# A recurrent attention and feed-forward kernel: a fifth slice of d_ff in plain float32, and a new order for the first 42 tasks

## The chip, the cores and the metric

The kernel runs on one core of a Trainium2 chip. The metric is the device time of one execution in microseconds (us). TensorE (PE) multiplies matrices into PSUM, VectorE (DVE) and ScalarE (ACT) work elementwise, GpSimd (POOL) does little here, and SyncE (SP) issues most of the DMA transfers.

## The reference

```python
# attention: r, k, v, w are (4, 8, 768, 48), u is (8, 48)
for t in range(S):
    cur = np.einsum('bhd,bhe->bhde', u[None] * kt, vt)
    y[:, :, t] = np.einsum('bhd,bhde->bhe', rt, state + cur)
    state = wt[:, :, :, None] * state + np.einsum('bhd,bhe->bhde', kt, vt)
# feed-forward on x = y as (3072 tokens, 384), d_ff = 2048
h = x @ w_in
g = h * (1.0 / (1.0 + np.exp(-1.702 * h)))
return (g @ w_out).astype(np.float32)
```

## The kernel before, in words

The 3072 tokens are 24 chunks of 128. A chunk `t` goes through 13 stages (`chunk`, written `a<t>` in the order below; each mention of the token runs one more stage):

1. DVE: a scan (L330) and a reciprocal; 2. DVE: a second scan (L335); 3. DVE: one multiplication that makes `kq` (L341); 4. PE: transposes of `k` (L348), ACT copies them out (`kt`, L350); 5. DVE: `rku` (L356, chunks 0 to 7) or three operations on `rk_t` (L359 to L361, later chunks); 6. PE: `ps_d` (L368, chunks 0 to 7); 7. ACT (chunks 0 to 7) or DVE makes `am`; 8. PE: `ps_u` (L398, L402); 9. the state: DVE, in a sequence's first chunk ACT copies `mid` first (L406); 10. DVE: two predicated copies into `am` (L415); 11. and 12. PE: `ps_y` (L425, L438), with a one-element copy between (L448); 13. ACT and DVE write the rows of `x`, as a high and a low half.

The feed-forward part is cut into 106 tasks, each a group of chunks by one slice of 128 columns of d_ff. `g<j>` is the first product of task j (PE, L502 to L504), `h<j>` its gelu (two activations on ACT, L519 and L520, and the subtraction `gl` on DVE, L522), `y<j>` its second product (PE, L540 to L542). Tasks 0 to 4 take slices 0 to 4 for the first pair of chunks (256 tokens), tasks 5 to 9 the same slices for the second pair, tasks 10 to 19 slices 5 to 9 for the two pairs in turn; from task 20 on a task has four chunks (512 tokens).

Ordinarily a number is split into two float32r halves and each product is three matmuls (high by high, low by high, high by low). For the tasks in `PLAIN` the product is one float32 matmul on the unsplit weights and an unsplit copy of `x` (`xw`, L497 and L537), and `h` is one activation on ACT with nothing on DVE.

The weights come in 12 pieces. `f<i>` fetches piece i (SP), and `w<i>` has four stages: 1. ACT: two activations (L253, L254); 2. DVE: two integer operations (L256, L259), after which the piece is a usable float32; 3. ACT: the high half (L263); 4. DVE: the low half (L267). Even pieces belong to the first product, odd ones to the second; pieces 0 to 3 hold slices 0 to 4 and a part of 5. The staging tile `st` has three buffers, so `f<i>` waits for stage 2 of `w<i-3>`.

`l<t>` loads chunk t's inputs on SP (chunk 0's second part on ACT's queue; later chunks also `rk_t`), `M` loads a small mask, `m<t>` is a measurement on ACT (L277), `x1`, `x3`, `x7` rearrange rows of `x` by DMA (L481, SP and POOL), `s0` splits `xw` for the tasks that are not plain, `u` loads one more constant. `d<n>` puts n matmuls on a constant tile (L305, 128x512 bf16) ahead of the next PSUM bank's real work; their results are overwritten.

Every engine runs its instructions in the order in which they were written, and that order is one string by hand, `RAMP`. It holds all work up to the second product of task 39, the gelu of task 41 included. After it `rest` orders what is left by a rule; that part is the same in both kernels, because both strings hold the same tokens (only the `d` differ). The edit is in two constants: `PLAIN`, which `plain` reads (L487), and `RAMP`, which the first of these loops reads.

```python
TASKS = [(0, c, c + 2, f) for c in (0, 2) for f in range(5)]
PLAIN = range(4)
for token in RAMP.split():
    do(token)
for token in rest():
    do(token)
```

Of the kernel before, what the change touches and what calls it, by code (L numbers as in the profile page):

```python
# [71 lines left out]

PLAIN = range(4)
WHOLES = range(2)
PARTS = [("a", -2, 2, 7), ("a", -1, 1, 7), ("a", 0, 1, 6), ("a", 1, 0, 5), ("a", 1, 1, 4),
         ("a", 1, 1, 7), ("a", 1, 2, 0), ("a", 1, 2, 3), ("a", 1, 2, 7), ("m", 1, 2, 7), ("a", 2, 1, 1),
# [1 line left out]
BEFORE = 9  # L80
FIRST = 42
RAMP = """
l0 l1 M l0 a0 a0 a0 f0 m0 d36 a0 a0 a0 a0 a1 a1 a1 m1 l0 d11 a0 a0 a0 w0 l2 a1 a1 d5 a1 a1 a2 f1 w1 w0 l1 d9 a1 a1
a1 a2 a0 l3 f2 a0 a2 a0 l3 a1 m2 d4 a2 a1 a1 a2 w2 a2 a2 a3 a3 l2 d9 a2 a3 x1 a3 a3 w1 m3 f3 a2 a3 g0 g1 h0 a3 w2 a2
y0 h1 a3 l4 a3 w3 f4 a3 a2 w1 f5 w2 a4 g2 a3 h2 a4 a2 w3 a3 w0 a2 a3 g3 s0 h3 a4 y1 y2 y3 w4 a4 a4 s0 a4 w2 w0 w4 a4
l5 l4 a4 g4 x3 h4 w3 w3 g5 w1 g6 g7 h5 g8 a5 w5 h6 w4 y4 y5 f6 f7 w4 g9 h7 w5 g10 w6 y6 a4 h8 y7 y8 w7 w6 h9 g11 w5
g12 y9 w5 h10 a5 f8 f9 g13 w6 h11 y10 y11 m4 a5 h12 w7 g14 l6 w6 l5 w8 f10 h13 a5 a5 y12 g15 g16 m5 h14 a4 h15 y13
a6 a5 w7 y14 y15 h16 g17 g18 w7 w9 y16 g19 w8 f11 h17 y17 w9 w8 h18 a6 w8 a5 h19 a4 l6 a5 w9 a5 a4 a6 a5 g20 w9 w10
h20 a6 y18 w10 w11 a6 w11 g21 h21 g22 l7 m6 y19 w10 w10 y20 w11 w11 a6 l8 a7 h22 a5 a4 l8 a7 a6 y21 a5 a7 a6 u g23
a6 l7 a6 a7 a7 l9 a8 h23 a7 a5 a7 g24 a6 l9 a7 a8 a7 a6 a8 m7 a7 a9 l10 a9 y22 a8 y23 a6 h24 a7 a8 a8 m8 a8 a8 a7 a7  # L90
a9 x7 g25 a8 h25 y24 y25 a9 a9 a10 g26 a8 l11 a10 a9 a9 a8 h26 l10 a9 a8 a10 m10 l12 a8 g27 a10 a9 a10 m9 h27 a11 a9
g28 g29 h28 a10 y26 h29 a9 a10 a11 l11 a10 a10 a9 a11 y27 y28 a10 a11 a11 y29 a11 a11 a9 m11 l13 a11 a11 a11 a10 a11
a10 a12 a11 a10 g30 a11 g31 g32 h30 h31 y30 a12 a12 m12 a13 g33 a12 h32 y31 y32 l14 g34 g35 g36 g37 a13 a13 h33 g38
h34 g39 h35 g40 y33 y34 h36 g41 h37 y35 y36 h38 y37 h39 h40 y38 h41 y39
"""
WIDE = 512
GAP = 64
# [7 lines left out]
def rwkv_ffn_kernel(ctx: ExitStack, tc, wkr, vp, vrk, ub, w_in, w_out, masks, vt, uc, out):  # L105
# [379 lines left out]
    def plain(j):  # L485

        return j in PLAIN  # L487

# [312 lines left out]
```

## Time and profile before

| | us |
|---|---|
| three runs | 510.77, 509.82, 505.54 |
| median | 509.82 |
| the profiled execution | 505.89 |
| its span, first to last instruction | 504.2 |
| outside the span | 1.7 |

The profile is one execution. Rows of a time line give the start, the duration, the engine (a `q` behind it is its sequencer, for instance a DMA issue), the line, the operation and the tiles (out, then in), the count, and in brackets the idle time of that engine just before with what ended it. Neighbouring instructions of one engine overlap a little, so from one start to the next is shorter than the duration.

### The profile page before, as it was taken

To read this page: it belongs to the slowest core of one execution; us is meant where nothing else is said; L and a number is where in the kernel's file an instruction comes from. 1 tells how busy PE (TensorE), PEld (TensorE's weight loads), DVE (VectorE), ACT (ScalarE), POOL (GpSimd) and SP (SyncE) were. 2 spreads that over 40 slices of the span, in tenths; PEclk is the share of its full clock that TensorE was granted. 3 is DMA by queue.
4 is the path that set the end of the run, shared out by engine and by line. 5 is a ranking of instruction groups with operands and counts; after the bars stand their busy time and mean duration, and the time that the engine had idled before them with its cause. 6 is when DMAs were issued, how large, how long until landed. Compare 5 with 4: busy or idle time off the path is not lost.

```text
span 504.2 us, 11925 instructions
## 1 busy us (share of the span) xinstructions
PE 492.4 (98%) x5064; PEld 406.1 (81%) x5064; DVE 294.8 (58%) x503; ACT 227.3 (45%) x527; POOL 15.4 (3%) x48
## 2 busy tenths in 40 slices
PE   9997999999999999999999999999999999999995
PEld 4676999887778888888888888888888878888884
DVE  8798999999896403755655555655555521111211
ACT  2897998865634313542342433342442432322221
POOL 2011000001001000000001000001000001000000
PEclk9999999999999999999999999999999999999999
DMA  8868586443731600171104071204040001100002
GB/s 222 252 185 228 171 211 192 107 128 109 214 105 24 167 0 2 63 219 45 55 1 126 17 213 61 59 1 128 2 156 1 1 1 31 64 0 1 0 0 72
DMA packets 26510, 45.84 MB, mean 91 GB/s; under 512 B 3952, under 2 KB 17712, under 8 KB 26448
## 3 DMA queue, kind: packets, MB, share of 16 engines
q1 hardware_dynamic: 25472, 42.94, 29.5%
q0 software_dynamic: 864, 1.66, 1.4%
q8 instruction: 42, 0.69, 0.6%
q10 hardware_dynamic: 112, 0.39, 0.3%
q14 instruction: 20, 0.16, 0.1%
HBM read 38.00 MB, written 4.72 MB: 85 GB/s over the span
## 4 chain that ended last, share of the span: by engine, by line
PE 89%; DVE 6%; DMA 2%; issue 1%; SPq 0%; ACT 0%; DVEq 0%
PE po L540 12%; PE ph L502 12%; PE ph L504 12%; PE ph L503 12%; PE po L542 12%; PE po L541 12%; PE ps_y L425 2%; PE ps_y L438 2%; PE ps_u L402 2%; PE ps_t L305 2%; PE ps_u L398 2%; PE ps_t L348 1%; PE ps_d L368 1%; DVE am L415 1%; DVE lp L335 1%
## 5 line engine op out<-in xcount | busy, mean ns | idle before, releaser
L522 DVE TENSOR_TENSOR gl<-gf,gh 128x512 fp32r<-128x512 f32 (+1 forms) x102 | 66.1, 648 | 160.4 <-ACT gf L520 159.2
L519 ACT ACTIVATE gh<-ph 128x512 fp32r<-128x512 f32 (+1 forms) x102 | 57.7, 566 | 204.6 <-PE ph L504 185.6
L502 PE MATMUL ph<-x,h 128*128 128x512 f32 (+1 forms) x306 | 116.1, 379 | 0.0
L504 PE MATMUL ph<-x,l 128*128 128x512 f32 (+1 forms) x306 | 114.2, 373 | 0.0
L503 PE MATMUL ph<-x,h 128*128 128x512 f32 (+1 forms) x306 | 114.1, 373 | 0.0
L540 PE MATMUL po<-gh,h 128*128 128x512 f32 (+1 forms) x300 | 114.0, 380 | 0.0
L542 PE MATMUL po<-gl,h 128*128 128x512 f32 (+1 forms) x300 | 112.2, 374 | 0.8 <-DVE gl L522 0.8
L541 PE MATMUL po<-gh,l 128*128 128x512 f32 (+1 forms) x300 | 111.9, 373 | 0.0
L504 PEld LDWEIGHTS ph<-x,l 128*128 128x128 f32 x306 | 57.6, 188 | 10.4
L542 PEld LDWEIGHTS po<-gl,h 128*128 128x128 f32 x300 | 56.5, 188 | 11.6 <-DVE gl L522 1.6
L502 PEld LDWEIGHTS ph<-x,h 128*128 128x128 f32 x306 | 57.7, 188 | 9.9
L503 PEld LDWEIGHTS ph<-x,h 128*128 128x128 f32 x306 | 57.7, 189 | 9.5
L540 PEld LDWEIGHTS po<-gh,h 128*128 128x128 f32 x300 | 56.5, 188 | 10.3
L541 PEld LDWEIGHTS po<-gh,l 128*128 128x128 f32 x300 | 56.6, 189 | 9.3
L520 ACT ACTIVATE gf<-ph 128x512 f32<-128x512 f32 (+1 forms) x102 | 57.3, 562 | 3.0 <-DVE gl L522 2.9
L330 DVE TENSOR_TENSOR_SCAN lp<-wkr_t,d1r 112x516 f32<-112x516 f32 x24 | 29.4, 1227 | 0.9 <-DMA wkr_t<-in_wkr 0.9
L335 DVE TENSOR_TENSOR_SCAN lp<-wkr_t,d1f 112x516 f32<-112x516 f32 x24 | 29.5, 1230 | 0.5
L341 DVE TENSOR_TENSOR kq<-wkr_t,lp 112x1024 f32<-112x1024 f32 x24 | 29.3, 1220 | 0.7 <-PE ps_y L438 0.3
L277 ACT ACTIVATE junk<-lp 112x1032 bf16<-112x1032 f32 x24 | 25.6, 1066 | 7.2 <-DVE lp L335 7.2
L350 ACT COPY kt<-ps_t 128x448 f32<-128x448 f32 (+1 forms) x24 | 12.7, 531 | 32.2 <-PE ps_t L348 32.0
L438 PE MATMUL ps_y<-kq,mid 64*64 64x64 f32 (+3 forms) x384 | 23.0, 218 | 3.4 <-issue 2.4
L438 PEld LDWEIGHTS ps_y<-kq,mid 48*48 48x48 f32 (+3 forms) x384 | 18.5, 127 | 4.6 <-issue 2.9
(102 smaller groups left out, 508.5 us busy)
## 6 DMA issues: line engine op xcount, KB each, us to landing
st<-in_w_out SPq DMA_DIRECT2D x6, 1024.0 KB, 6.3
rk_t<-in_vrk SPq DMA_DIRECT2D x16, 384.0 KB, 3.9
st<-in_w_in SPq DMA_DIRECT2D x6, 896.0 KB, 7.0
v_t<-in_vrk SPq DMA_DIRECT2D x24, 192.0 KB, 3.5
out_t<-ob SPq DMA_DIRECT2D x15, 256.0 KB, 2.2
wkr_t<-in_wkr SPq DMA_DIRECT2D x18, 192.0 KB, 2.9
wkr_t<-in_wkr SPq DMA_DIRECT2D x36, 96.0 KB, 3.5
wkr_t<-in_wkr SPq DMA_DIRECT2D x5, 577.9 KB, 6.4
```

The costliest lines, as they stand in the source:

```text
L330: V.tensor_tensor_scan(li[:, ::-1], w1[:, ::-1], d1r.rearrange("r p c -> r (p c)")[:, ::-1], 0.0, op0=ALU.mult, op1=ALU.add)
L335: V.tensor_tensor_scan(pm, w0, d1f.rearrange("r p c -> r (p c)"), 0.0, op0=ALU.mult, op1=ALU.add)
L438: T.matmul(ps[b][head(h), p], from_[head(half), p * D + OFF * h : p * D + HB], qf[head(half), p, blocks[b]], start=False, stop=p == PAIRS[ ...
L502: T.matmul(ph, h_, xs[i][:, 0, c, cs], start=c == 0, stop=False)
L503: T.matmul(ph, h_, xs[i][:, 1, c, cs], start=False, stop=False)
L504: T.matmul(ph, l_, xs[i][:, 0, c, cs], start=False, stop=c == NM - 1)
L519: A.activation(gh, ph, AF.Gelu_apprx_sigmoid, scale=1.0 / W_SCALE)
L520: A.activation(gf, ph, AF.Gelu_apprx_sigmoid, scale=1.0 / W_SCALE)
L522: V.tensor_tensor(gl, gf, gh.bitcast(F32), op=ALU.subtract)
L540: T.matmul(o, h_, gh, start=first, stop=False, skip_group_check=True)
L541: T.matmul(o, l_, gh, start=False, stop=False, skip_group_check=True)
L542: T.matmul(o, h_, gl, start=False, stop=f == NF - 1, skip_group_check=True)
```

## The change

`PLAIN` goes from four tasks to five, so task 4 (slice 4, first pair of chunks) becomes a plain float32 task. `RAMP` is another sequence of the same 395 working tokens. The constant matmuls go from 36 + 11 + 5 + 9 + 4 + 9 = 74 to 26 + 6 + 6 + 5 + 4 + 5 = 52. In the diff the beginning, a middle part and the end of the two strings:

```diff
-PLAIN = range(4)
+PLAIN = range(5)
 RAMP = """
-l0 l1 M l0 a0 a0 a0 f0 m0 d36 a0 a0 a0 a0 a1 a1 a1 m1 l0 d11 a0 a0 a0 w0 l2 a1 a1 d5 a1 a1 a2 f1 w1 w0 l1 d9 a1 a1
-a1 a2 a0 l3 f2 a0 a2 a0 l3 a1 m2 d4 a2 a1 a1 a2 w2 a2 a2 a3 a3 l2 d9 a2 a3 x1 a3 a3 w1 m3 f3 a2 a3 g0 g1 h0 a3 w2 a2
-y0 h1 a3 l4 a3 w3 f4 a3 a2 w1 f5 w2 a4 g2 a3 h2 a4 a2 w3 a3 w0 a2 a3 g3 s0 h3 a4 y1 y2 y3 w4 a4 a4 s0 a4 w2 w0 w4 a4
...
-g28 g29 h28 a10 y26 h29 a9 a10 a11 l11 a10 a10 a9 a11 y27 y28 a10 a11 a11 y29 a11 a11 a9 m11 l13 a11 a11 a11 a10 a11
-a10 a12 a11 a10 g30 a11 g31 g32 h30 h31 y30 a12 a12 m12 a13 g33 a12 h32 y31 y32 l14 g34 g35 g36 g37 a13 a13 h33 g38
...
+l0 M l1 l0 a0 a0 a0 d26 a0 l0 a1 a0 d6 a0 f0 m0 a0 a0 l2 a1 l1 a1 l2 a0 a1 m1 a1 d6 a1 l3 a1 a0 a2 a1 a0 a1 a0 a1 w0
+l3 a2 a1 a0 a2 a3 d5 a2 a1 a1 f1 w1 f2 x1 a2 a3 d4 a2 a3 a2 a2 l4 a3 a2 a3 d5 a3 w0 f3 a3 a3 a2 a3 m2 a3 g0 h0 g1 w2
+l4 w1 a2 h1 a3 w2 a4 a2 f4 w3 a2 w2 w3 a3 a3 x3 y0 y1 w2 g2 g3 h2 w1 h3 f5 g4 w0 h4 a4 s0 y2 w4 w0 y3 y4 m3 g5 s0 a4
+w4 h5 w3 w1 a4 w3 a4 w5 g6 h6 g7 g8 g9 l5 w5 h7 y5 f6 w4 l6 f7 w4 a4 a4 a4 h8 a5 w5 y6 f8 w5 y7 h9 a5 w6 g10 g11 g12
...
+a7 m7 a6 m6 a8 g24 a7 a7 a5 a8 y22 a7 h24 a6 a7 a7 a6 a7 l8 a8 y23 l9 a7 a6 a8 l9 a8 m8 a8 a7 l10 a9 a8 l10 a8 a7 a7
+a9 x7 a9 g25 y24 h25 y25 a9 a9 a8 a8 a10 a10 g26 g27 h26 y26 a9 a9 l11 h27 a8 a9 a9 m9 a8 a10 g28 a11 y27 a9 a10 a10
+a10 a10 g29 a8 a11 h28 a9 a10 l11 a9 a11 h29 y28 a10 a11 y29 g30 a11 a9 a11 m10 a10 a11 a11 a11 a11 h30 l12 a10 a11
...
```

## Rows read from the trace of the kernel before

**Rows 1.** The page: busy time of each engine over the whole span.

```profile
PE 492.4 (98%) x5064; PEld 406.1 (81%) x5064; DVE 294.8 (58%) x503; ACT 227.3 (45%) x527; POOL 15.4 (3%) x48
```

**Rows 2.** Windows: stretch, length, busy (instructions) by engine, granted clock, DMA share, GB/s.

```profile
0.00:5.00 5.00, 3.86 (x10) 1.38 (x11) 2.97 (x5) 1.49 (x2) 3.13 (x24) 1.00 0.63 168
5.00:10.00 5.00, 5.00 (x23) 2.22 (x22) 4.64 (x6) 1.16 (x2) 0.00 (x0) 1.00 1.02 266
40.00:45.00 5.00, 2.57 (x77) 2.08 (x78) 4.86 (x5) 1.76 (x5) 0.00 (x0) 1.00 1.06 311
60.00:80.00 20.00, 19.70 (x166) 19.50 (x165) 19.80 (x31) 18.57 (x39) 0.00 (x0) 1.00 0.70 182
140.00:155.00 15.00, 14.22 (x343) 11.60 (x342) 12.66 (x30) 4.34 (x12) 0.00 (x0) 1.00 0.23 71
155.00:201.00 46.00, 46.00 (x230) 37.63 (x225) 17.13 (x26) 15.88 (x35) 1.50 (x3) 1.00 0.21 52
180.00:200.00 20.00, 20.00 (x90) 16.56 (x89) 3.77 (x6) 6.52 (x12) 0.00 (x0) 1.00 0.01 1
```

**Rows 3.** Time line of DVE, the end of chunk 11's stage 10.

```profile
152.62 0.76 DVE L415 COPY_PREDICATED am<-after,ps_u 128x256 f32<-128x256 int32 x2
```

**Rows 4.** Time line of DVE, chunks 0 and 1: first scan, `rku`, second `kq`, state.

```profile
5.25 1.23 DVE L330 TENSOR_TENSOR_SCAN lp<-wkr_t,d1r 112x516 f32<-112x516 f32 x1 [0.94 <-DMA wkr_t<-in_wkr]
...
9.14 0.68 DVE L356 TENSOR_TENSOR rku<-wkr_t 112x512 f32<-112x512 f32 x1
12.49 1.23 DVE L341 TENSOR_TENSOR kq<-wkr_t,lp 112x1024 f32<-112x1024 f32 x1
16.33 0.36 DVE L412 TENSOR_TENSOR sf<-ps_u,mid 112x192 f32<-112x192 f32 x1 [2.61 <-ACT mid L406]
```

**Rows 5.** Time line of PE: the first constant matmuls and what follows them.

```profile
1.14 10.11 PE L305 MATMUL ps_t<-warm 128*128 128x512 bf16 x36 [1.14 <-DVE warm L119]
11.09 0.55 PE L348 MATMUL ps_t<-ident,kq 112*128 112x112 f32 x4
```

**Rows 6.** Time line of ACT, 8 to 16 us.

```profile
8.07 1.06 ACT L277 ACTIVATE junk<-lp 112x1032 bf16<-112x1032 f32 x1 [5.29 <-DVE lp L335]
11.68 0.53 ACT L350 COPY kt<-ps_t 128x448 f32<-128x448 f32 x1 [2.45 <-PE ps_t L348]
...
12.73 2.02 ACT L378 ACTIVATE am<-same,s 128x64 f32<-128x64 f32 x8
14.66 1.05 ACT L277 ACTIVATE junk<-lp 112x1032 bf16<-112x1032 f32 x1
15.98 0.32 ACT L406 COPY mid<-ps_u 112x192 f32<-112x192 f32 x1 [0.18 <-PE ps_u L402]
```

**Rows 7.** Time line of SP's queue: chunk 1's load and the mask.

```profile
1.29 0.41 SPq L198 DMA_DIRECT2D wkr_t<-in_wkr  x1
2.80 0.31 SPq L617 DMA_DIRECT2D hm<-in_masks  x1
```

**Rows 8.** The instructions of one line: whole loads of a chunk, from issue to landing.

```profile
DMA to landing us min/median/max: 4.6/6.4/11.0
```

**Rows 9.** Time line of PE and DVE, 43 to 56 us: waits before the split tasks begin.

```profile
43.92 0.25 PE L438 MATMUL ps_y<-kq,mid 48*48 48x64 f32 x1 [2.43 <-issue]
46.25 1.49 DVE L272 TENSOR_TENSOR x<-ps_y,x 112x256 fp32r<-112x256 f32 x4 [1.28 <-ACT x L271]
55.95 2.36 DVE L267 TENSOR_TENSOR l<-h,h 128x1024 fp32r<-128x1024 f32 x2 [0.51 <-ACT h L263]
```

**Rows 10.** Time line of DVE: chunk 10's `rk_t` operations begin.

```profile
137.54 0.56 DVE L359 TENSOR_TENSOR rk_t<-rk_t 128x384 f32<-128x384 f32 x1 [1.56 <-DMA rk_t<-in_vrk]
```

**Rows 11.** The chain that ended last, pieces in time: start, duration, what.

```profile
46.86 3.88 PE po L537 x18
53.57 0.12 PE ph L502
```

**Rows 12.** Groups of instructions by line and form: DVE's subtraction for 256 tokens.

```profile
L522 DVE TENSOR_TENSOR gl<-gf,gh 128x256 fp32r<-128x256 f32 x16 | 6.7, 416 | 0.1
```

More of the change, by code (lines that the diff above doesn't have):

```diff
@@ L82 @@
 RAMP = """
-l0 l1 M l0 a0 a0 a0 f0 m0 d36 a0 a0 a0 a0 a1 a1 a1 m1 l0 d11 a0 a0 a0 w0 l2 a1 a1 d5 a1 a1 a2 f1 w1 w0 l1 d9 a1 a1
-a1 a2 a0 l3 f2 a0 a2 a0 l3 a1 m2 d4 a2 a1 a1 a2 w2 a2 a2 a3 a3 l2 d9 a2 a3 x1 a3 a3 w1 m3 f3 a2 a3 g0 g1 h0 a3 w2 a2
-y0 h1 a3 l4 a3 w3 f4 a3 a2 w1 f5 w2 a4 g2 a3 h2 a4 a2 w3 a3 w0 a2 a3 g3 s0 h3 a4 y1 y2 y3 w4 a4 a4 s0 a4 w2 w0 w4 a4
-l5 l4 a4 g4 x3 h4 w3 w3 g5 w1 g6 g7 h5 g8 a5 w5 h6 w4 y4 y5 f6 f7 w4 g9 h7 w5 g10 w6 y6 a4 h8 y7 y8 w7 w6 h9 g11 w5
-g12 y9 w5 h10 a5 f8 f9 g13 w6 h11 y10 y11 m4 a5 h12 w7 g14 l6 w6 l5 w8 f10 h13 a5 a5 y12 g15 g16 m5 h14 a4 h15 y13
@@ L88 @@
[L88 to L91, printed above, removed]
-g28 g29 h28 a10 y26 h29 a9 a10 a11 l11 a10 a10 a9 a11 y27 y28 a10 a11 a11 y29 a11 a11 a9 m11 l13 a11 a11 a11 a10 a11
@@ L93 @@
-a10 a12 a11 a10 g30 a11 g31 g32 h30 h31 y30 a12 a12 m12 a13 g33 a12 h32 y31 y32 l14 g34 g35 g36 g37 a13 a13 h33 g38
-h34 g39 h35 g40 y33 y34 h36 g41 h37 y35 y36 h38 y37 h39 h40 y38 h41 y39
+l0 M l1 l0 a0 a0 a0 d26 a0 l0 a1 a0 d6 a0 f0 m0 a0 a0 l2 a1 l1 a1 l2 a0 a1 m1 a1 d6 a1 l3 a1 a0 a2 a1 a0 a1 a0 a1 w0
+l3 a2 a1 a0 a2 a3 d5 a2 a1 a1 f1 w1 f2 x1 a2 a3 d4 a2 a3 a2 a2 l4 a3 a2 a3 d5 a3 w0 f3 a3 a3 a2 a3 m2 a3 g0 h0 g1 w2
+l4 w1 a2 h1 a3 w2 a4 a2 f4 w3 a2 w2 w3 a3 a3 x3 y0 y1 w2 g2 g3 h2 w1 h3 f5 g4 w0 h4 a4 s0 y2 w4 w0 y3 y4 m3 g5 s0 a4
@@ new lines @@
+w4 h5 w3 w1 a4 w3 a4 w5 g6 h6 g7 g8 g9 l5 w5 h7 y5 f6 w4 l6 f7 w4 a4 a4 a4 h8 a5 w5 y6 f8 w5 y7 h9 a5 w6 g10 g11 g12
+h10 y8 y9 a5 y10 h11 w6 w7 h12 w6 a4 w6 y11 a4 a5 a5 g13 h13 g14 f9 y12 w7 m4 g15 l5 a5 w8 h14 a4 w8 h15 w7 a5 w7
+g16 g17 y13 a6 h16 y14 y15 y16 w9 a6 h17 w9 f10 f11 g18 g19 m5 h18 a5 w8 a4 a5 h19 a5 w8 w10 y17 a6 l7 w9 y18 y19
+w11 g20 a7 l7 w9 a6 a6 w10 h20 g21 g22 w11 h21 w10 l6 w11 a6 a6 y20 w10 w11 a4 h22 u y21 g23 a7 h23 a5 a6 a6 a5 l8
+a7 m7 a6 m6 a8 g24 a7 a7 a5 a8 y22 a7 h24 a6 a7 a7 a6 a7 l8 a8 y23 l9 a7 a6 a8 l9 a8 m8 a8 a7 l10 a9 a8 l10 a8 a7 a7
@@ L95 @@
+a9 x7 a9 g25 y24 h25 y25 a9 a9 a8 a8 a10 a10 g26 g27 h26 y26 a9 a9 l11 h27 a8 a9 a9 m9 a8 a10 g28 a11 y27 a9 a10 a10
+a10 a10 g29 a8 a11 h28 a9 a10 l11 a9 a11 h29 y28 a10 a11 y29 g30 a11 a9 a11 m10 a10 a11 a11 a11 a11 h30 l12 a10 a11
+l13 a10 a10 a11 y30 a12 a12 m11 a11 g31 a12 l14 a13 a13 g32 g33 h31 g34 y31 g35 g36 h32 h33 h34 a13 m12 y32 h35 g37
+a12 y33 h36 y34 y35 y36 h37 y37 g38 g39 g40 h38 g41 h39 h40 y38 y39 h41
 """
```

## The prediction

> **What bounds the kernel now.** I read the page first: PE is busy for 98% of the span [rows 1]. That alone says little about the ramp, because constant matmuls and matmuls that wait inside a burst count as busy too. The windows by stage say more [rows 2]. From 155 to 201 us PE has no gap at all (46.00 of 46.00), and what follows RAMP is written in the same order in both kernels. So the time changes by as much as the instant changes at which PE is through with RAMP, at about 201 us. In the ramp itself PE is not what is short: in 60 to 80 DVE is busy 19.80 of 20 us, and in 40 to 45 PE works 2.57 of 5 us while DVE works 4.86.
>
> Next I looked for the place where DVE hands over. Chunk 11's predicated copies on DVE end at 152.62 + 0.76 = 153.4 [rows 3]. Behind them stands chunk 11's `ps_y` on PE, and after it PE never stops. RAMP's end is therefore 153.4 plus about 47 us of PE work that stands behind this point. Two things can move it: DVE comes to this point earlier, or less PE work stands behind it. DVE comes earlier if it has less to do ahead of it or waits less; the waits are in the time line of DVE [rows 4, 9, 10].
>
> **Fifth plain slice.** A plain product shows as two records. The 18 records of three second products take 3.88 us, 0.216 each [rows 11], so the 6 products of task 4 take 12 x 0.216 = 2.59. As a split task they were 18 matmuls of 0.12 [rows 11], 2.16. PE pays +0.43. It does so at about 45 us in the new order, where by the walk below PE waits for DVE anyway; I take 0, and 0.43 if that cover is gone. DVE loses one `gl`, 0.42 long, some 0.33 net of the overlap [rows 12]: -0.33. ACT loses one activation, which is not on the path.
>
> [...]
>
> **Fewer constants.** The 36 constants run from 1.14 to 11.25, and chunk 0's transposes start at 11.09 [rows 5], though `kq` was ready at 9.14, where DVE goes on to `rku` [rows 4]. In 0 to 5 us ten constants take 3.86 us, 0.39 apart; in 5 to 10 us 23 take 5.00, 0.217 apart [rows 2]. [...] Ten fewer of the late kind end at 11.25 - 2.17 = 9.08: the transposes start at 9.14, 1.95 earlier. The other 12 constants taken out (2.6 us of PE) stood where PE waits for DVE; I take 0 for them, and -2.6 at most.
>
> **Order of chunks 0 and 1.** DVE finishes chunk 1's `kq` at about 13.6 in both orders (the same work from the first scan at 5.25 on) and then waited 2.61 us, until 16.33, for ACT's copy of `mid` [rows 4]. That copy stood at 15.98 behind eight `am` (12.73 to 14.66) and behind chunk 1's measurement (14.66 to 15.9) [rows 6]. In the new order: transposes at 9.14, `kt` copied by 10.2 (11.09 to 12.11 before), then chunk 0's measurement until 11.4 (it used to fill an empty ACT at 8.07, now it lies under the wait for `ps_d`). `rku` now follows chunk 1's first scan on DVE, done at 11.1, so `ps_d` ends at about 11.9; the six constants before it (9.5 to 10.8) are over by then. `s` and `am` take 12.48 to 14.66, 2.2 us, before, so they end at 14.2; `mid` follows at once, as chunk 1's measurement now comes after it. DVE goes on at 14.6: it waits 1.0 in place of 2.61, -1.7 with the overlap.
>
> **Chunks 2 and 3, and the weights.** Before, pieces 0 to 3 stand between the stages of chunks 2 and 3, so chunk 3's `x` comes late: PE waits 2.43 at 41.5, DVE 1.28 for ACT's `x` and 0.51 for ACT's high half [rows 9]. The new order runs the chunks first, the weights behind. ACT's `w3` waits for its fetch, whose buffer comes free at about 30 us, so I leave 0.5 of these 1.8 us: -1.3 (from 0 to -1.8).
>
> **Queues.** `M` now stands ahead of `l1` on SP, and it can't issue before 2.80 [rows 7]. So `l1` goes from 1.29 to about 3.15; whole loads land after 4.6, in the median 6.4 and at worst 11.0 us [rows 8], so at 7.8 to 14.2, and DVE needs it at 9.14. The fetch and `v` now stand behind it, so I take near the short end: +0.1 (0 to 5). `l2` issues when `rku` is done, about 11.1, and is needed at 16.2: +0.3 (0 to 6, by the same rows). `x3` stands ahead of `f5` and holds it until chunk 3's `x` is there, some 5 us later than its buffer would; `w5` on ACT and the gelus behind it wait, PE has other tasks: 0. Chunk 10's `rk_t` load moves ahead of `x7` and of the first stores on SP: DVE's wait of 1.56 [rows 10] goes, -1.56 (0 at the worst).
>
> **PE work behind chunk 11.** The first product of task 30 (nine matmuls; 90 take 20.00 us [rows 2], so 0.222 each, 2.0 us) moves from behind chunk 11's copies to ahead of them. That would be -2.0. But task 26's gelu moves behind chunk 10's two scans, and counted the same way it allows about 1 us less than chunk 11 does, so I take -1.0 (from 0 to -2.0).
>
> **Sum.** -0.33 - 1.7 - 1.3 + 0.1 + 0.3 - 1.56 - 1.0 = -5.5 us. All good ends without the 12 constants give -7.4, with them -10. All bad ends of the small terms give about -1; a load at its worst more. For an execution like the profiled one that is 505.89 - 5.5 = 500.4. Two of the three runs lie 4 to 5 us above it and the median 3.9, so against the median it is 509.82 - 5.5 = 504.3.
>
> **Rivals.** *The head start is given back.* DVE has the same work but one `gl`, and in 60 to 80 it idles 0.2 us of 20 [rows 2]: any new wait on it between 50 and 150 us goes straight to the end. Another sequence can have other waits, for a fetch behind `x3` or for ACT behind a weight piece. If 3.5 of the 5.5 come back, the time is 507.8; this case spans -0.5 to -3.5. Against it: PE is further ahead of DVE than before, so DVE waits for it less.
>
> [...]
>
> [...]
>
> *More than that.* The 12 other constants also count and task 26 does not bind: -7.5 to -10, about 501.
>
> That the change is not what it says I can rule out: `range(5)` makes task 4 plain, for the first pair of chunks; slice 4 of the second pair (task 9) stays split, so "pairs" is too wide, and the sum above has one task alone.
>
> **How the numbers follow.** The forecast (-3.5 to -7.5, so 502.3 to 506.3 against the median) gets 0.56, the head start given back 0.30, more than that 0.09, the lower clock 0.05. A measurement of this kernel can tell about 1% from no change, here 5.1 us. Of the forecast's 0.56 about 0.38 lie beyond that, as its middle is -5.5: faster 0.38 + 0.09 = 0.47, the same 0.18 + 0.30 = 0.48, slower 0.05. The range must also hold the level on which the runs fall: from the lowest run less 7.0 (498.5) to the median less 0.5 (509.3); that leaves out the clock and the ends of the others.
>
> **What would show it.** Transposes at 9.1; DVE's wait for `mid` 1.0; no wait of DVE for `x` near 40 us; the first plain product at about 30; no wait at chunk 10's `rk_t`; chunk 11's copies ended at about 149; PE without a gap from there to about 195.5; granted clock 1.00. It is wrong if the copies still end after 152 (given back), if `l1` or `l2` ends a wait of DVE of over 1 us, or if the clock falls below 1.00 before 50 us.

## The result, and the profile after

The changed kernel takes 502.54 us in the median of 17 runs (501.08 to 508.14), the kernel before 509.65 beside it. The ratio is 0.9897, with a 95% interval from 0.9868 to 0.9925 over the executions that nothing else disturbed, which leaves out one of the kernel before at 1255.17 us: 3.8 to 6.7 us less, in the middle 5.2. The two medians lie 7.1 us apart. The forecast was -5.5 us and 504.3 us, so the change came out nearly as it was put and the median 1.8 us lower. The steps did not come out: two of them missed in opposite directions, and the rest of this document is about them.

The page after, busy time of each engine (it answers to [rows 1]):

```profile
PE 489.3 (98%) x5036; PEld 405.8 (81%) x5036; DVE 294.2 (59%) x502; ACT 227.2 (45%) x526; POOL 15.4 (3%) x48
```

Windows after: stretch, length, busy (instructions) of each engine, granted clock, DMA share, GB/s [rows 2]:

```profile
0.00:5.00 5.00, 3.86 (x11) 1.42 (x12) 2.97 (x5) 1.49 (x2) 3.13 (x24) 1.00 0.61 140
5.00:10.00 5.00, 4.21 (x22) 2.00 (x21) 4.62 (x5) 0.00 (x0) 0.00 (x0) 1.00 0.99 285
30.00:35.00 5.00, 4.54 (x73) 3.75 (x74) 4.76 (x10) 3.89 (x14) 0.00 (x0) 0.69 0.81 254
40.00:45.00 5.00, 5.00 (x25) 4.41 (x24) 4.70 (x9) 4.74 (x15) 0.00 (x0) 1.00 0.14 31
60.00:80.00 20.00, 19.32 (x199) 18.96 (x199) 19.24 (x28) 17.93 (x43) 0.00 (x0) 1.00 0.74 222
155.00:201.00 46.00, 46.00 (x266) 37.94 (x266) 19.18 (x31) 16.52 (x35) 1.50 (x3) 1.00 0.23 54
```

Three rows matter below. In 40 to 45 PE works all 5 us where it worked 2.57. In 30 to 35 the granted clock is 0.69 on the mean: at about 31.9 it fell to 0.50 for 3.4 us (0.50 on the mean in 32 to 35). In 60 to 80 PE and DVE have gaps of 0.68 and 0.76 us, where they had 0.30 and 0.20. For 30 to 35 the window of the kernel before is:

```profile
30.00:35.00 5.00, 5.00 (x89) 4.42 (x88) 4.76 (x8) 4.77 (x18) 0.18 (x1) 1.00 0.66 213
```

Time line of PE after: the first constants, chunk 0's transposes, the first plain products, and the second product of task 39, near RAMP's end [rows 5, 9]:

```profile
1.14 7.46 PE L305 MATMUL ps_t<-warm 128*128 128x512 bf16 x26 [1.14 <-DVE warm L119]
9.39 0.57 PE L348 MATMUL ps_t<-ident,kq 112*128 112x112 f32 x4 [0.79 <-DVE kq L341]
31.62 4.51 PE L497 MATMUL ph<-l,l 128*128 128x256 f32 x12 [0.33 <-DVE am L415]
196.18 0.39 PE L540 MATMUL po<-gh,h 128*128 128x512 f32 x1
```

The transposes start at 9.39 in place of 11.09, and now it is `kq` that they wait for. The first twelve records of plain products take 4.51 us. In a profile of e8 below, where the granted clock stays at 1.00, the same twelve take 2.75, so the lower clock (0.50 in 32 to 35) costs PE some 1.8 us. The same instruction of task 39 started at 198.60 before. The two rows, of e8 and of the kernel before:

```profile
32.73 2.75 PE L497 MATMUL ph<-l,l 128*128 128x256 f32 x12
```

```profile
198.60 0.39 PE L540 MATMUL po<-gh,h 128*128 128x512 f32 x1
```

Time line of DVE after [rows 3, 4, 9, 10]:

```profile
10.52 0.66 DVE L356 TENSOR_TENSOR rku<-wkr_t 112x512 f32<-112x512 f32 x1
...
14.84 0.36 DVE L412 TENSOR_TENSOR sf<-ps_u,mid 112x192 f32<-112x192 f32 x1 [1.25 <-ACT mid L406]
...
36.89 1.23 DVE L256 SCALAR_TENSOR_TENSOR st<-st 128x1024 int32<-128x1024 int32 x1 [1.27 <-ACT l L254]
...
138.67 0.55 DVE L359 TENSOR_TENSOR rk_t<-rk_t 128x384 f32<-128x384 f32 x1
...
152.37 0.76 DVE L415 COPY_PREDICATED am<-after,ps_u 128x256 f32<-128x256 int32 x2
```

The wait for `mid` is 1.25 in place of 2.61, and chunk 10's `rk_t` no longer waits for its load. Yet chunk 11's copies end at 153.13, 0.26 us earlier than before. So DVE's shorter waits bring almost nothing at this point. Where the time went is in the list of DVE's waits up to 153 us after (who waited, for whom: us in total, times, the longest):

```profile
DVE mid L409 <- PE ps_u L402: 2.1, 3, 1.1
DVE gl L522 <- ACT gf L520: 1.8, 5, 0.5
DVE sf L412 <- ACT mid L406: 1.5, 2, 1.3
DVE st L256 <- ACT l L254: 1.3, 1, 1.3
DVE mid L448 <- PE ps_y L438: 1.1, 1, 1.1
```

The two lines at which DVE waits for PE, L409 and L448, made up 0.9 us before; the fourth line is new. The sum is put together below.

### The profile page after: what moved, and what is told of

Its sections match the earlier page's. It is cut to its first block, busy times and chain, and to the rows that moved or that the text cites. A ratio compares the mean times of both kernels' runs of the same rounds, so it can differ in the third digit from the quotient of the medians.

```text
span 501.6 us, 11866 instructions
## 1 busy us (share of the span) xinstructions
PE 489.3 (98%) x5036; PEld 405.8 (81%) x5036; DVE 294.2 (59%) x502; ACT 227.2 (45%) x526; POOL 15.4 (3%) x48
## 4 chain that ended last, share of the span: by engine, by line
PE 87%; DVE 8%; DMA 2%; issue 1%; ACT 1%; SPq 0%; DVEq 0%; ACTq 0%
PE po L540 12%; PE ph L502 12%; PE ph L504 12%; PE ph L503 12%; PE po L542 12%; PE po L541 12%; PE ps_y L438 2%; PE ps_y L425 2%; PE ps_u L402 2%; PE ph L497 2%; PE ps_u L398 2%; DMA wkr_t<-in_wkr 2%; PE ps_t L348 2%; PE po L537 1%; DVE lp L330 1%
## 5 line engine op out<-in xcount | busy, mean ns | idle before, releaser
L502 PEld LDWEIGHTS ph<-x,h 128*128 128x128 f32 x303 | 57.0, 188 | 10.8 <-PE po L542 0.9
L504 PEld LDWEIGHTS ph<-x,l 128*128 128x128 f32 x303 | 57.0, 188 | 10.4
L503 PEld LDWEIGHTS ph<-x,h 128*128 128x128 f32 x303 | 57.1, 188 | 9.6
L540 PEld LDWEIGHTS po<-gh,h 128*128 128x128 f32 x297 | 55.9, 188 | 10.4
L481 POOL DMA_DIRECT2D x<-x x18 | 9.0, 507 | 380.1 <-DVE x L272 269.2
```

The source lines that it names most:

```text
L502: T.matmul(ph, h_, xs[i][:, 0, c, cs], start=c == 0, stop=False)
L503: T.matmul(ph, h_, xs[i][:, 1, c, cs], start=False, stop=False)
L504: T.matmul(ph, l_, xs[i][:, 0, c, cs], start=False, stop=c == NM - 1)
L540: T.matmul(o, h_, gh, start=first, stop=False, skip_group_check=True)
```

## A ledger for every run: where the time is set

One reading turned out to hold in all profiles and carries most of what follows. The windows from the start to the end of chunk 11's copies give DVE's busy time (third pair of columns); what is missing to the length is its waits. Before, after, and three experiments (e1, e11 and e9, in this order, one view each):

```profile
0.00:153.39 153.39, 147.01 (x2094) 121.44 (x2094) 139.36 (x217) 107.61 (x268) 8.28 (x34) 1.00 0.63 175
```

```profile
0.00:153.13 153.13, 146.18 (x2075) 122.81 (x2075) 138.74 (x216) 107.43 (x267) 8.28 (x34) 0.99 0.64 175
```

```profile
0.00:157.00 157.00, 150.52 (x2094) 123.98 (x2094) 139.35 (x217) 107.64 (x268) 8.28 (x34) 0.98 0.60 171
```

```profile
0.00:155.24 155.24, 145.38 (x2066) 122.54 (x2066) 138.84 (x216) 106.70 (x265) 8.28 (x34) 0.98 0.63 173
```

```profile
0.00:161.40 161.40, 149.82 (x2103) 125.15 (x2103) 138.92 (x216) 107.30 (x267) 8.28 (x34) 0.98 0.60 166
```

DVE's work up to this point hardly changes; its waits do. From the end of the copies to task 39's second product the distance is the same (within 0.1 us) in every profile of one tail, and from there to the end lie 305.3 to 306.2 us in all. So each span is DVE's work + its waits + this distance + about 305.5. Each row of the table is one execution; those of e6 and e9 are the longest of their kernels.

| kernel | copies end | DVE's work | DVE's waits | from there to task 39 |
|---|---|---|---|---|
| before | 153.39 | 139.36 | 14.03 | 45.21 |
| e1, before again | 157.00 | 139.35 | 17.65 | 45.16 |
| e5, 26 constants first | 151.74 | 139.32 | 12.42 | 45.15 |
| e7, `f5` late | 156.11 | 139.34 | 16.77 | 45.17 |
| e10, before shifted | 155.51 | 139.33 | 16.18 | 45.17 |
| e12, plain slice alone | 153.61 | 138.90 | 14.71 | 45.17 |
| e3, old head, new tail | 158.80 | 139.80 | 19.00 | 43.06 |
| e2, new head, old tail | 157.80 | 138.79 | 19.01 | 45.19 |
| after | 153.13 | 138.74 | 14.39 | 43.05 |
| e4, 5 constants more | 153.85 | 138.50 | 15.35 | 43.03 |
| e8, 12 constants more | 153.44 | 138.56 | 14.88 | 43.04 |
| e9, e8 shifted | 161.40 | 138.92 | 22.48 | 43.06 |
| e6, four plain slices | 164.07 | 139.12 | 24.95 | 43.03 |
| e11, task 30 put back | 155.24 | 138.84 | 16.40 | 45.10 |

Three things can be read off. The new tail is worth 2.1 us in every case. DVE's work is 138.50 to 138.92 with five plain slices and 139.12 to 139.80 with four. The waits vary by microseconds from one kernel to the next, and from one execution of the same kernel to the next (before and e1).

## Experiments

**e1, the kernel before once more (no edit).** The kernel before has runs from 505.5 to 507.6 and from 509.4 to 510.8 us. This was to show what parts them.

> The kernel before, unchanged, for the clock and span of each of its executions, which the times of before don't list. Theory A (its executions differ because the granted clock falls in some of them): those near 505.5 us show clock 1.000 and a span near 504, those near 510 show 0.99 to 0.995, about 3.4 us of half clock or more. Theory B (the spread has another cause): clock 1.000 in nearly all, whatever the time. Ratio to before 1.00 by both.

507.82 us (504.41 to 510.20, 12 runs), ratio 0.9998 [0.9963, 1.0032]: six runs from 504.4 to 506.9, six from 508.7 to 510.2. The mean granted clock of each run bears out Theory A. The five runs at 0.999 or 1.000 take 504.4 to 506.1 (505.5 on the mean), the five at 0.990 to 0.993 take 509.5 to 510.2 (509.8), and the two at 0.994 lie between, at 506.9 and 508.7. The profiled run is one of the long ones, 509.48. Its time line of PE:

```profile
44.45 0.34 PE L438 MATMUL ps_y<-kq,mid 48*48 48x64 f32 x1 [2.52 <-issue]
```

and its windows:

```profile
40.00:45.00 5.00, 2.48 (x54) 1.93 (x54) 4.90 (x7) 1.69 (x2) 0.00 (x0) 0.90 1.05 311
45.00:50.00 5.00, 5.00 (x44) 4.32 (x41) 3.28 (x7) 3.60 (x13) 1.10 (x3) 0.50 0.57 135
```

The stop of PE that [rows 9] show with 2.43 is here 2.52, and behind it the clock is granted at 0.50; DVE is busy 3.28 of 5 us there. The copies end 3.6 us later than in the profile of before, all of it waits. The largest is a wait that the profile of before does not have (time line of DVE):

```profile
58.58 0.42 DVE L522 TENSOR_TENSOR gl<-gf,gh 128x256 fp32r<-128x256 f32 x1 [2.70 <-ACT gf L520]
```

So the profile on which the prediction was built was one of the short executions. In this long one PE goes on 0.5 us later than there, and some 3.1 us more come behind the fall of the clock.

**e2 and e3, the two halves of the new order, each with the other half of the old.** e2 takes the new order up to its fourth `w3` and five plain slices, then the rest in the old order; e3 the old order up to its fourth `w1`, then the rest in the new one, with four. First the edit of e2, then that of e3, each against the kernel before, cut to the ends of the exchanged parts.

```diff
-PLAIN = range(4)
+PLAIN = range(5)
...
-l0 l1 M l0 a0 a0 a0 f0 m0 d36 a0 a0 a0 a0
...
+l0 M l1 l0 a0 a0 a0 d26 a0 l0 a1 a0 d6 a0
...
+w4 h5 w3 w1 a4 w3
```

```diff
-a6 l9 a7 a8 a7 a6 a8 m7 a7 a9 l10 a9
...
+a8 y23 l9 a7 a6 a8 l9 a8 m8 a8 a7 l10
...
```

> The new order up to the point where weight pieces 0 to 3 are split (the w3 after the first two stages with h5), with task 4 plain and all of the new constants; from there on what is left, in the old order. My theory (head start of 3 us, the rest from the later order): about -3.0 us, 506.6 against a median of 509.65. Rival 1 (the head is all of it): -5.2, 504.4. Rival 2 (the later order is all of it): 509.5.

> The old order and the old constants up to the same point (weight pieces 0 to 3 split), four plain tasks; from there on what is left, in the new order. My theory (later order worth 2.5 us: less PE work behind chunk 11, no wait for chunk 10's rk_t): about -2.5 us, 507.1. Rival 1 (the head is all): 509.5. Rival 2 (the later order is all): 504.4.

e2: 510.45 us, ratio 1.0063 [1.0036, 1.0089]; e3: 512.12 us, 1.0088 [1.0049, 1.0127]. Both halves alone are slower than either whole, which neither theory had. In e2 PE waits at the seam for a `rku` that the old order makes late, and the wait for `rk_t`'s load is back (time line of PE, then of DVE):

```profile
55.69 1.65 PE L368 MATMUL ps_d<-hm,rku 112*128 112x2 f32 x7 [4.76 <-DVE rku L356]
```

```profile
141.94 0.56 DVE L359 TENSOR_TENSOR rk_t<-rk_t 128x384 f32<-128x384 f32 x1 [2.09 <-DMA rk_t<-in_vrk]
```

An order written out by hand can't be cut at any place; as measurements of a half these runs are worth little. What survives the seam is the ledger's last column: 45.19 with the old tail, 43.06 with the new.

**e4 and e8, hold the clock in the new order.** More constants where it fell: 5 in e4 (first edit), 12 in e8 (second), each against the kernel after.

```diff
-d5 a3 w0 f3 a3 a3 a2 a3 m2 a3 g0 h0
+d5 a3 w0 f3 a3 d3 a3 a2 a3 m2 a3 d2 g0 h0
```

```diff
-d5 a3 w0 f3 a3 a3 a2 a3 m2 a3 g0 h0
+d9 a3 w0 f3 a3 d4 a3 a2 a3 m2 a3 d4 g0 h0
```

> The new kernel with 3 constant matmuls more ahead of chunk 3's ps_u and 2 more ahead of the first plain product (57 in place of 52), where the profiled execution after fell to half clock for 3.4 us. Theory A (thin PE work around 28 to 32 us lets the clock fall, and that costs by a late gelu and a late weight piece): fewer executions below clock 1.000 and a median of about 501.5, 1 us under the changed kernel. Rival (constants only add PE time, or 5 are too few to hold it): the same clocks and 502.5 to 503.5.

> The new kernel with 12 constant matmuls more: 9 in place of 5 ahead of chunk 3's ps_d, 4 ahead of its ps_u, 4 ahead of the first plain product (64 in place of 52). Theory A (more PE work between 26 and 32 us holds the clock; 5 more were too few): no clock below 1.000 between 25 and 40 us in the trace, the first two plain products at full pace, DVE's wait of 1.3 us for ACT behind the late gelu gone, median 501 to 502. Rival (constants do not hold it, or they delay chunk 3 by as much as they save): the clock falls as before, or median 502.5 to 504.

e4: 502.51 us, ratio 0.9913 [0.9884, 0.9942], and the clock still falls (0.71 in 30 to 35; the twelve records take 3.75 us). e8: 504.6 us in 6 runs, 0.9917 [0.9885, 0.9948]; in its profile the clock stays at 1.00 up to the copies and far beyond. Chunk 6's copies start at 106.57 in e8 and at 107.81 in the kernel after, 1.24 us apart. That is what is left when the price of the 12 constants is paid: they hold up the first plain product by 1.1 us (32.73 and 31.62), so that the first gelu starts hardly earlier (34.23 and 34.32). In this profile the gain did not arrive, because PE stops later (time line of PE of e8):

```profile
120.48 0.50 PE L503 MATMUL ph<-x,h 128*128 128x512 f32 x1 [2.29 <-issue]
```

So holding the clock is worth 1.2 us up to chunk 6, and as times e4, e8 and the kernel after can't be told apart.

**e5, the first constants alone.**

```diff
-l0 l1 M l0 a0 a0 a0 f0 m0 d36 a0 a0
+l0 l1 M l0 a0 a0 a0 f0 m0 d26 a0 a0
```

> The kernel before with 26 in place of 36 first constant matmuls, nothing else. My step (chunk 0's transposes start at 9.1 in place of 11.1, ACT's copy of mid about 2 us earlier, and DVE, which sets the pace to 153 us, keeps that): the transposes at 9.1 in the trace, DVE's wait for mid under 1 us in place of 2.61, median 1.5 to 2 us under the kernel before. Rival (what is saved at 16 us is waited for again before 60 us, because PE stops at 41 us for something that does not depend on it): 0 to -0.5 us.

507.47 us, ratio 0.9979 [0.9956, 1.0002], about -1.1 us, with an interval that just holds no change. The mechanism is there in full: DVE's wait for `mid` falls from 2.61 to 1.11 without any other edit (time line of DVE of e5), and the copies end 1.65 earlier.

```profile
14.97 0.36 DVE L412 TENSOR_TENSOR sf<-ps_u,mid 112x192 f32<-112x192 f32 x1 [1.11 <-ACT mid L406]
```

**e6, the new order with four plain slices.** Task 4's products and gelu move behind the steps that split its weights.

```diff
-PLAIN = range(5)
+PLAIN = range(4)
...
-h3 f5 g4 w0 h4 a4 s0 y2 w4 w0 y3 y4 m3 g5 s0 a4 w4 h5 w3 w1 a4 w3 a4
+h3 f5 w0 a4 s0 y2 w4 w0 y3 m3 g5 s0 g4 a4 w4 h5 h4 w3 w1 a4 w3 y4 a4
```

> The new order and constants with four plain tasks: task 4 is split again, so its first product and gelu stand behind the split of xw and its second product behind the w3 that makes piece 3's low half. My step (the fifth slice is worth 0.33 us of DVE and nothing else): 502.5 to 503. Rival (the fifth slice is what PE has to do between 43 and 49 us, before any split task can start): PE idle there by about 2.6 us more and the median 1 to 2.5 us above the changed kernel.

511.0 us, ratio 1.0044 [1.0019, 1.0068], 1.5% above the kernel after. The profiled run is the longest of the 12, 514.31. In it PE waits 3.48 us at 54.3 for ACT's high half, as the split of task 4's weights isn't done when `y4` comes:

```profile
57.77 0.57 PE L540 MATMUL po<-gh,h 128*128 128x256 f32 x1 [3.48 <-ACT h L263]
```

and 4.42 us near 29 lie behind a piece of the weights that landed late (below). The first is a seam of my making, so e12 does it without one.

**e12, the fifth plain slice alone, in the old order.**

```diff
-PLAIN = range(4)
+PLAIN = range(5)
```

> The kernel before with the fifth plain slice alone, everything in the old order. By the prediction's sum DVE loses 0.33 us and PE pays 0.43: 0 to -0.4 us, ratio 0.999 to 1.000. Rival, from e6 (the new order with four plain slices, 1.5% slower than with five): the plain slice also takes the split of its weights and ACT's activation out of the way, which would bring several us here too: 0.99 or below. If it comes out near 1.000, e6's loss lies in its seam and in the order, not in the slice.

508.07 us, ratio 1.0001 [0.9968, 1.0034]. DVE's work falls by 0.46 (139.36 to 138.90), and its waits grow by 0.68. By itself the slice brings nothing that can be measured. That in the new order it lets task 4 stand as early as it does is how the order was written; with e6's seam, no run shows what that is worth.

**e7, piece 5's load behind `x3`, and e10, other positions in PE's code.** Both ask what stops PE at 41.5 us in the old order. e7 takes the load out of the stretch in which the DMA engines are full (share 1.06 in 40 to 45 [rows 2]). e10 exchanges 13 wide constants for 56 narrow ones (128x128): 86 instructions more. In the kernel before the 4 and the 9 wide ones take 1.04 and 2.10 us; in e10's profile the 20 and the 36 narrow ones take 1.29 and 3.69, the 36 where the granted clock is 0.66 (30 to 35). The edit of e7, then that of e10.

```diff
-f4 a3 a2 w1 f5 w2 a4 g2 a3
+f4 a3 a2 w1 w2 a4 g2 a3
...
-a4 g4 x3 h4
+a4 g4 x3 f5 h4
```

```diff
-m2 d4 a2 a1 a1 a2 w2 a2 a2 a3 a3 l2 d9 a2
+m2 n20 a2 a1 a1 a2 w2 a2 a2 a3 a3 l2 n36 a2
...
-cold.append((i, WIDE // P if kind == "d" else 2))
+cold.append((i, WIDE // P if kind == "d" else 1))
```

> The kernel before, with the fetch of weight piece 5 (1 MB) issued behind x3 in place of ahead of it, so at about 50 us in place of 37. Theory A (PE's stop of 2.43 us at 41.5 is a fetch of its own instructions, in the trace from 40.75 on, that is late because the DMA engines are full of weight fetches from 30 to 45 us; the stop is what lets the clock fall to half at 44 us in about every second execution): the stop shrinks under 0.5 us, no execution below clock 0.998, median 504 to 505.5 us and little spread. Rival (the stop has another cause): it stays near 2.4 us and the spread of 504 to 510 stays.

> The kernel before with 13 wide constants near 25 and 28 us exchanged for 56 narrow ones of 3 us in all: 86 more instructions on PE ahead of 31 us. Theory, code fetch: the boundary of 256 instructions moves from inside chunk 3's x products (41.3) to about 39.1, where the 256 instructions ahead of it took 6.0 us and not 4.25. PE's stop of 2.43 us at 41.5 is gone or under 0.6 us; with it the fall of the clock behind it (44 to 51), so that the times lie on the lower of this kernel's two levels: median 2 to 3.5 us shorter, ratio 0.993 to 0.996. A smaller stop near 141 would take 0.5 back. Rival, the stop belongs to these products or to the full DMA engines: it stays between the same kind of rows, 1.7 to 3.7 us long, and the ratio is 1.000.

e7: 509.13 us, ratio 1.0004 [0.9984, 1.0024]; e10: 506.46 us, 0.9961 [0.9927, 0.9995]. In neither is the stop gone. Time line of PE of e7, then of e10:

```profile
45.04 0.25 PE L438 MATMUL ps_y<-kq,mid 48*48 48x64 f32 x1 [3.74 <-issue]
```

```profile
44.10 1.24 PE L497 MATMUL ph<-l,l 128*128 128x256 f32 x5 [1.65 <-issue]
```

In e10 it lies at another piece of work, between two plain products and not among chunk 3's `x` products. What it kept is its place in PE's code. Counted in PE's records (matmuls and weight loads, and the few of its sequencer), the stop comes after number 1217 in all seven profiles with the old head: before, e1, e3, e5, e7, e10, e12 (in e5 the profile names ACT as what ended it). The windows give the same: 600 matmuls and 600 weight loads ahead of it in six of them, 600 and 601 in e10. The later stops, in e3, e8 and e9, come after number 3009 or 3265, and so do two shorter ones of 0.7 and 0.5 us, in e4 and e6 after 3265. These counts are 7 and 1 times 256 apart. And each of the twelve stops ends 1.36 to 1.61 us after a block of 16,384 bytes has landed on the queue that the trace calls "instruction": before, the block lands at 42.41 and PE goes on at 43.92; e7, 43.53 and 45.04; e10, 42.49 and 44.10; e8, 118.90 and 120.48. I read this as PE waiting there for its own code: the place in the count and the landing just ahead of it speak for it in all twelve, though no run changed the transfer itself. That e10's better spacing would remove the stop was wrong: it had 5.4 us for the 256 instructions, and the block started 4.6 us after the first of them. Its time is 0.4% shorter all the same; in its profile the clock falls near 30 us (0.66 in 30 to 35) and not behind the stop (1.00 in 40 to 45), and what made the other runs shorter isn't shown.

**e9, e8 with other positions in PE's code.** Five wide constants for 21 narrow ones, 32 instructions more.

```diff
-l4 a3 a2 a3 d9 a3 w0 f3
+l4 a3 a2 a3 d4 n21 a3 w0 f3
```

> The same work and order as e8, with five of its wide constants (128x512) exchanged for 21 narrow ones (128x128) of the same length together: 32 more instructions on PE ahead of 30 us, no more time. In all profiles so far PE's unexplained stops lie behind its recorded instructions 1216, 3008 and 3264, which are 7 and 1 times 256 apart, and each ends 1.4 to 1.6 us after a block of 16,384 bytes has landed on the instruction queue. Theory, code fetch: PE stops where it uses up 256 instructions faster than the next block comes. In e8 such a stop of 2.29 us lay at 118.2, where 256 instructions took 2.2 us; 32 instructions earlier the 256 ahead of the boundary took 4.9. So the stop goes: PE's row at 118 to 120.5 without a wait on issue, y39 2.3 us earlier than in e8, span about 499.6, ratio to the kernel before about 0.987. Rival, the stop belongs to product 25 or to chance: it stays or moves anywhere, ratio 0.992 as in e8.

506.78 us, ratio 0.9962 [0.9932, 0.9993]: a miss, 0.0045 above e8's. In its profile the stop at task 25's product went and two others came, after numbers 3009 and 3265 again (time line of PE of e9):

```profile
121.97 0.50 PE L540 MATMUL po<-gh,h 128*128 128x512 f32 x1 [1.37 <-issue]
...
127.82 0.27 PE L438 MATMUL ps_y<-kq,mid 64*64 64x64 f32 x1 [1.16 <-issue]
```

This profile is of the longest of the 13 runs, 511.65, so it does not tell what the median lost. Most of what it lost itself has another cause. ACT's first step on the weight piece that is issued at about 19 us, in the kernel after, in e11 and in e9 (one time line each):

```profile
25.25 1.18 ACT L253 ACTIVATE st<-st 128x1024 int32<-128x1024 uint32 x1 [0.97 <-DMA st<-in_w_out]
```

```profile
27.53 1.17 ACT L253 ACTIVATE st<-st 128x1024 int32<-128x1024 uint32 x1 [2.96 <-DMA st<-in_w_out]
```

```profile
29.33 1.17 ACT L253 ACTIVATE st<-st 128x1024 int32<-128x1024 uint32 x1 [5.02 <-DMA st<-in_w_out]
```

The load was issued at 18.91, 19.68 and 18.94, so it took some 6.3, 7.8 and 10.4 us. Nothing ahead of it differs between the first two kernels, so its time varies by itself by some 1.5 us. Behind this step on ACT stands chunk 2's copy `s`, for which PE (0.71 us at 30.13 in the kernel after) and then DVE wait. Over six profiles of the new order DVE's waits rise with it: 0.97 (after) with 14.39, 1.05 (e8) with 14.88, 2.15 (e4) with 15.35, 2.96 (e11) with 16.40, 4.74 (e6, with its seam) with 24.95, 5.02 (e9) with 22.48. That is a relation over profiles; no run changed the load alone. This weak spot is new: in the old order pieces 0 to 3 stood between other stages. It was not tried to take it away.

**e11, task 30 alone put back.**

```diff
-y29 g30 a11 a9 a11 m10 a10 a11 a11 a11 a11 h30 l12 a10 a11 l13 a10 a10 a11 y30 a12 a12 m11 a11 g31 a12
+y29 a11 a9 a11 m10 a10 a11 a11 a11 a11 l12 a10 a11 l13 a10 a10 a11 a12 a12 m11 g30 a11 g31 h30 a12
...
-h31 g34 y31
+h31 y30 g34 y31
```

> The kernel after, with task 30 alone put back: its first product ahead of chunk 11's last step (as in the kernel before), its gelu and second product behind it in turn. Theory: the nine products of 0.222 us ahead of chunk 11's copies are the 2.0 us by which PE has less to do behind them; put back, they stand behind the copies again, PE has no other work in their place and task 39's second product starts 2.0 us later: ratio 0.4% above the kernel after's 0.9897, about 0.994. Rival: PE has no room there, so that DVE's copies come 2 us earlier without them: no change, 0.990. In between it shows how much of the 2.0 was real (the prediction took 1.0).

504.84 us, ratio 0.9923 [0.9892, 0.9953], 0.0026 above the kernel after's; the intervals overlap, so the times alone don't settle it. The rows do. Time line of DVE of e11, then of PE:

```profile
154.48 0.76 DVE L415 COPY_PREDICATED am<-after,ps_u 128x256 f32<-128x256 int32 x2
```

```profile
200.34 0.39 PE L540 MATMUL po<-gh,h 128*128 128x512 f32 x1
```

From 155.24 to 200.34 it is 45.10, the value of the old tail, where the kernel after has 43.05. This one task is 2.05 of the tail's 2.1 us. Its copies end 2.1 us later than the kernel after's, but that is the late load above (2.96 in place of 0.97), so the rival, that without the nine products DVE's copies would come earlier, has nothing for it.

## Why the prediction was right or wrong

**The time: right, though not by its sum.** The sum put -4.5 us on DVE's side and -1.0 on PE's. In the two profiles DVE's side gave -0.26 (work -0.62, waits +0.36) and PE's -2.16, with -0.2 behind task 39: -2.6 us of span, 504.2 to 501.6. So the agreement is in part luck. By the prediction's own signs two of three went against it: the copies ended at 153.13, after its 152, and the clock fell before 50 us. Only the third did not come: no load of chunks 1 or 2 ended a long wait of DVE.

**Constants: right.** The transposes at 9.39, the wait for `mid` at 1.25 (forecast 1.0), and e5 shows that ten constants by themselves do that. What it is worth at the end can be read off runs at like clock: e5's two runs at 0.998 or more take 505.2 where the six of the kernel before beside it take 506.7, and those below 0.994 take 508.2 (six) and 510.2 (ten). That is 1.4 and 2.0 us, near the forecast 1.7.

**Plain slice: right in DVE's work**, -0.33 forecast and -0.46 in e12's profile; there its waits grew by more, and the time did not change.

**Chunks 2 and 3 (-1.3): half.** PE's stop at 41.5 and DVE's wait of 1.28 behind it are gone (5.00 of 5 us in 40 to 45). But the reason was another: PE stopped there after number 1217, as read above for its code and not for chunk 3's work. In the new order the same number, 1217, is passed at 38.6 with its block landed at 36.8. DVE's new wait of 1.27 at 36.89 takes the place of the old one. It waits for ACT's step on a weight piece, which stands behind task 0's gelu, and this gelu waited 1.08 us for the products under the lower clock. In e8, where the clock held but constants stood ahead of these products, the wait is still 0.98 (time line of DVE):

```profile
36.83 1.23 DVE L256 SCALAR_TENSOR_TENSOR st<-st 128x1024 int32<-128x1024 int32 x1 [0.98 <-ACT mid L448]
```

**The clock: wrong.** It was to stay at 1.00 and fell at about 32 us to 0.50, behind the stretch from 20 to 32 in which PE works 10.37 of 12 us; before, where it stayed at 1.00, PE works 11.36 of them. My walk had found no wait of PE above 1.3 us and took that as safe. The chance of 0.05 for a lower clock was an estimate of mine. What the fall cost was some 1.8 us of PE work, and 1.2 at chunk 6. It does not fall in every execution: the 3.4 us at 0.50 in the profile take 0.003 off the mean clock, and eight of the 17 runs have a mean of 0.998 or more. In the profiles of the new head it fell six times in seven (0.96 to 0.99 on the mean up to the copies), with 5 more constants too (e4), and held at 1.00 only with 12 more (e8); as much in e9 did not hold it in the profile (0.67 in 30 to 35), behind the late load, though ten of its 13 runs have a mean of 0.998 or more.

**`rk_t` (-1.56): the wait went, its time did not.** The row at 138.67, chunk 10's, has no wait, but DVE waits 2.1 us in all at L409 and 1.1 at L448, both for PE, where it waited 0.9 before. From 100 us to the copies' end DVE's busy time falls from 48.30 of 53.39 to 46.52 of 53.13: 1.5 us more of waiting, 6.6 in place of 5.1. That is the rival "the head start is given back", with PE and not a fetch or ACT as the main releaser: PE works 51.68 of these 53.13 us, and the new order gives it work ahead of what DVE needs.

**Task 30 (-1.0): too small.** It is -2.05 (e11). I let task 26's gelu limit it, on an estimate that had no row; PE shows no gap between 155 and 201. This is the term that was mis-sized.

**The level of the runs: the step that failed unseen.** I set the sum against one profile and carried it over to the median unchanged, as if the 3.9 us between them belonged to both kernels alike. They go with a fall of the clock, which both kernels have in some of their executions. The kernel before at a mean clock of 0.999 or 1.000 takes 505.5 us (e1, five runs), at 0.990 to 0.993 it takes 509.8 (five). The kernel after takes 502.0 at 0.998 to 1.000 (eight runs, 501.1 to 502.8), 503.8 at 0.994 to 0.997 (seven), and 508.1 at 0.989 and 0.991 (two). So at a clock that holds the change is worth about 3.5 us, and the other 1.7 or so of the 5.2 would be that fewer of its executions fall far: two of 17, and five of e1's 12. This compares runs of two sessions, as the runs of before that stand beside the result have no clock on record.

The two profiles hide it the other way round: before at 1.000 stands against after at 0.995. They differ by 2.5 us; with the 1.2 of e8 added it is some 3.7, near the 3.5. Of the 3.5, 2.1 are the tail and 0.6 DVE's work, which leaves 0.8 for waits.

**What stays open.** Why the block of 16,384 bytes comes late: it starts 3.7 us after the count of 256 before it in the kernel before, 4.6 in e10 and 5.2 in e7, each with a DMA share of 1.0 to 1.1 from that count to its start. But in the kernel after it is 2.3 with a share of 1.00, in e8 at 117.7 it is 2.0 with 0.81, and in e3 at 116.3 and e9 at 119.5 it is 3.7 and 3.6 with 0.36 and 0.35. So the load on the DMA engines alone does not explain it; and e7 took one load away and the block came later still. Also open is why the clock falls behind some stops (2.52 in e1, 3.74 in e7) and not behind others (2.43 before, 2.17 in e12).

## What to carry to other kernels

Split the span at the point where one engine hands over for good, and keep a ledger of that engine's work, its waits and the distance to the end: here the gains in waits ahead of the point were eaten by other waits (14.03 us in all before, 14.39 after), and the 2.1 us less work behind it stayed in every profile of the new tail. Before a sum is set against a median, find out what parts the runs, and compare runs at like clock: a profile of a short execution hides what a change may remove. And where an engine stops with "issue" as the releaser, count its instructions up to there before blaming the work at that place.

## What the runs showed of the hardware

That PE might wait for its own code was not expected at all. It is my reading of twelve stops of 1.2 to 3.7 us in nine profiles, which come after instruction numbers that differ by multiples of 256 and end about 1.5 us after a 16,384-byte block lands. The one of 2.43 us in the kernel before comes where PE gets through some 256 small matmuls and weight loads in 4.3 us (37.0 to 41.3).

A load of 1 MB let ACT go on 6.3, 7.8 and 10.4 us after its issue (issued at 18.9, 19.7 and 18.9, ACT at 25.25, 27.53 and 29.33) in three profiles of nearly the same order.
